# Group sums in parts, two tiles written in parts, and a new written-out order in a two-layer spectral-filter and GLU kernel

## The chip, the cores and the metric

The kernel runs on one core of one Trainium2 chip. The metric is the device time of one execution in microseconds (us), and a kernel's time is the median of several runs. Before the change the median of three runs is 1050.22 us (1048.97 to 1051.25).

The engines are named as the profile names them: PE is TensorE, DVE is VectorE, ACT is ScalarE, POOL is GpSimd, SP is SyncE, which only issues transfers here.

## The reference

Two kinds of layer alternate, twice each, on `x` of 2048 x 512 numbers in float32:

```
x = x + A(layernorm(x))    A: X = rfft2(x) over both axes; X = X * (w_r + 1j * w_i); irfft2(X)
x = x + B(layernorm(x))    B: ((x W_gate) * (x W_up)) W_down,  512 -> 1792 -> 512
x = x + A(layernorm(x))
x = x + B(layernorm(x))
```

The same weights serve both times. The change is in A; B fills most of the time.

## The kernel before

`x` is kept on chip in `xs`, as 16 tiles of 128 x 512. "Layer 0" and "layer 1" below are the first and the second pair of A and B.

A transforms in stages. **Tiles.** For each of the 16 tiles, VectorE or ScalarE computes the layernorm's mean and spread, ScalarE scales the tile's transform matrix by it (`tws` in layer 0, `tw` in layer 1), and TensorE makes the tile's product `tp` (`fwd_rest`, L469). The result goes into a big array E of 128 x 4 x 16 x 16 x 8: blocks, tiles, groups, columns of a group. Tiles marked "P" in `FOLD` are halved ahead by GpSimd (`fo`), and ScalarE copies their product to E in one 128x512 copy. Tiles marked "Q" (2, 5, 8, 11 and 14 of layer 0) are halved after the product: ScalarE copies one half to `tb`, and VectorE writes the sum and the difference with `tb` to E, 128x256 each. Tile 15 is copied in two parts, the columns of groups 0 and 1 (64) first or last and those of groups 2 to 15 (448), which `cuts` in `fwd_rest` says.

**Groups.** E is then read across the tiles. For each of the 16 groups, `middles` (L529) makes two sums `fs`: halves of E added and subtracted, 128x256 each, read for all 16 tiles. So the first sum of a group needs all 16 tiles in E. Groups 0 and 1 (`FAST`) are summed by VectorE, the others by GpSimd. TensorE multiplies them (`dp`, eight 64x128 products for each group, two records each in the profile), ScalarE copies the result (`zs`), TensorE transforms again (`zp`), VectorE and GpSimd multiply with the filter (`wq`, loaded by SyncE; GpSimd adds a 128x8 correction to each piece), TensorE transforms back (`vq`), and ScalarE copies it into E over the group. Groups go to TensorE in the sets of `TWOS`: 0 alone, then pairs. **Inverse tiles.** Then each tile is transformed back (`yi`, `yo`), added to `xs`, normalised (`xn`) and transposed (`tq`) for B, whose products `gx` to `gz`, `ex` to `ez` and `db` fill TensorE for hundreds of microseconds. Layer 1's tile products run largely woven into layer 0's B.

What sets the order: every operation is first recorded in a list with what it reads and writes, and `Plan.order` (L268) then replays that list in the order of a table, `ORDER`, which a program has worked out ahead and which is stored compressed; `PLACES` gives each temporary its buffer. The instructions of one engine run in that order, and an instruction waits until the engines that it depends on have got far enough. So a wait at the head of an engine's queue also holds what stands behind it. Buffers are rings: 18 temporaries of 128 x 512, eight banks for the results of products. Every instruction is issued through one helper class, `Queue`, whose line, L314, is therefore the line of nearly every row of the profile; rows are told apart by the tiles that they name.

At the start TensorE runs `WARM` (6) idle products of 128x512 and one of 128x256 on zeros (`wp<-warm`), before the first tile is ready. Between tiles and groups it runs one more idle product (`idle`, L524, `wp<-midt`).

Of the kernel before, what the change touches and what calls it, by code (L numbers as in the profile page):

```python
# [103 lines left out]
FAST = (0, 1)  # L104
TWOS = [(0,)] + [(g, g + 1) for g in range(1, 15, 2)] + [(15,)]
# [14 lines left out]
    'mA)yv(X1R#89tT6z8G{oKwKY`m8|JQq}s|Jy^QYX^$ziAf}Eu~S|;mQaq-#7^JV3A?IBBamF&>lL^xKe$!ebI!tUF&BmOKZ(d<!@`>oL?PA2O6*q5*2_$V9Sox<;KuUJXsbAnXonO-uE'  # L120
    '7|hiX@~WN*-<f+&`%6QaLR{nVew4(6u%hy`t_E52Z3k0@?;~}tRAi^W_&ZYP5H0uZE)q}bE4n~Rf$Cha6e}+BcXfo0XHA?$fUvQ6>nmL^ZS_}auFK>XeOiu#gl2qpnGquy`jYODJniN!'
    '@Qd)iTOI-V&zWrdI~dL)I?js;nrL=wDZMOJiFpYvYNBPGz9n0bP)BBKNj)m<q^>NpSJ0{pIQ|?&wUc_}%_e(Hx|^SEJGo$+g{1p?^ny3pPvc1=Ps$f)_!)WD7lf_TDq6(cw5`p2ogs5{'
    'g;oH4ZKXdr>?yBkKVq4o=WKanvExattmTczlMA#Pk=mwT%0fNPZe64dE9Ynn*~-6CGD<hda6To;e~8Z`(nE&u-hw)CRp#4z(v&QHR?d6(@_Vt1uc7*o36%r3mT8BCwHhXcw754^U)81('
    '#+7;IE89(mT4UNsbJ;F&`n^6Ztz|4Za$RDH%#Ru>7D?gKU3!6z2~?NGVDJMpy>InK{Sj1bCF>W7hXr+AKFCz<jE6hubZM-!C5`V#L2+eJc|bQwD}4&7i$G{aDMH4$JBPI~Pv(+=A##M*'
    'AISJwGE{%ngLqA~J6d_fC=<l&(HHRFU1WvhgJ|ORv>ql#xAZH#QW34%;)!9%OC%#U>ML?kBjf>Dtk20OSh!P%@ccI2E^ksP7DyzL?_pVnyst0GcSw1Ty7CY8?hP=Lt5?yrF<JMXHs|$0'
    'RwPh$rh@(t@k2#y*$$>kn7g3AusPsYFs=p{lL5r3C4TnM@isVeahz|q+D*FEPB2@@*@L#Ec~(|n?=eaD8<|`QQ7cPBM&+H9)3yp8J*r8@w}m8EA~Z|GOg^8lkt5~gjFi`fwxJhE-tW*n'
    '`P<f&({j(om}D~co)pkO@$3V}uy&6vYS#JfyaTqO$)|pO4qC#&%VrHVp5{w^WOguXeZ{}k$=Rto9Di=r>MCZg|E{?pLXWA4{Nj3pI$&6nq6a|YaT{gwY?3K0SM;<^Hs>_gRyAkU+NNd~'
    'NchfHGV~W4XCm?W4f}{mCmW7xaV<>+z9c#J7P1;3bGbeWR`aQt*QqV>`1vCB<OV&*Ros<20klSG1UsFuC%D#KmXUL1Kwku}M$V9lE2%?2bLV#(Z?=*Pk>q3-d04)&E#-4+tI(<Hm^_`w'
    'y7Tr0JHl&4hs~!tAJd`!Chre+iUsFC+a4xSrrOud8`?kznf=5tLyuV_Pf!7jq?#u3G4I3h-WufAmf3i?HI=m{$SWuL_BlJtt10D(<`ytuWIa{*wk`oL>-8BrO9cKtL!2tmy(UW^`?z@;'
    'l#T%xe-gLFc8FQ4Ep;Uo>`Sc$#+KN>wY^!QFVj!9YgwYuMJC%(cv}3UUPrE7VTV;j?{BJ58mR3@CrJdW4}p%pGSH4OY5F*t46tL(Hgr%>U61FUk!S2eb3(_nq9YyuPd!IGE@&I_cR2|B'  # L130
    'UYk)1%gbBXJJ2{=dfO-&V^-657TO#zw#}^9_w6|Doxqb;Pm+Hz=<={s*0r*cI$cC+5TBED;j>6@DQmcv4Enm#VV3G;JJg)UYs>M@DRo@rq<&!MnLgCPM%1ULOm#ZJCOUfx{9`5^us>IS'
# [1055 lines left out]
```

## Time and profile before

| | us |
|---|---|
| median of 3 runs (lowest, highest) | 1050.22 (1048.97, 1051.25) |
| profiled execution: its own time | 1049.96 |
| profiled execution: span of the records | 1048.2 |
| busy in the span: PE matmul | 1032.4 |
| PE weight load | 900.8 |
| DVE | 803.6 |
| POOL | 747.0 |
| ACT | 421.0 |

The span runs from the first to the last record; the execution's own time has 1.76 us more around it. Busy time is summed over the records of an engine; weight loads run beside products, so PE's two shares overlap. In the timelines a row is a run of like instructions: start, time from the first start to the last end, engine, what is written `<-` what is read, the shape, how many (`x4`), and in brackets how long the engine stood idle before it and what released it. The tables of stretches also give PEclk, the granted clock of TensorE as a share of full speed; it is 1.00 in every stretch shown.

### The profile page before, as it was taken

Reading aid. Unit: us, or ns where it says so; the run is one execution under the profiler, and the core shown is the slowest. Engines: PE = TensorE matmul, PEld = TensorE weight load, DVE = VectorE, ACT = ScalarE, POOL = GpSimd, SP = SyncE. Lnnn points to the kernel's source line nnn. Section 1 sums busy time; section 2 is a strip of 40 time slices with the busy share of each in tenths; the row PEclk is TensorE's granted clock in tenths of the full one; section 3 lists DMA queues with packets and bytes.
Section 4 is the critical chain, followed back from the end, with each engine's and each line's share of the span. In section 5 each row is a group of like instructions: output and inputs, shape, how many; then the busy total and the mean of one; then the engine's idle time right before and its main releaser. Section 6 shows DMA issues by size and latency. Waiting matters only on the chain.

```text
span 1048.2 us, 18805 instructions
## 1 busy us (share of the span) xinstructions
PE 1032.4 (98%) x6560; PEld 900.8 (86%) x6560; DVE 803.6 (77%) x1581; ACT 421.0 (40%) x1011; POOL 747.0 (71%) x960
## 2 busy tenths in 40 slices
...
GB/s 360 224 83 191 64 218 229 234 214 277 253 213 140 278 215 158 201 164 230 120 319 78 6 12 201 153 176 176 190 275 219 91 222 220 162 211 179 213 141 81
DMA packets 129469, 193.66 MB, mean 185 GB/s; under 512 B 39264, under 2 KB 50784, under 8 KB 127328
## 3 DMA queue, kind: packets, MB, share of 16 engines
...
q14 instruction: 41, 0.34, 0.1%
...
## 4 chain that ended last, share of the span: by engine, by line
PE 90%; DVE 6%; POOL 1%; ACT 1%; DMA 1%; issue 1%; SPq 0%; DVEq 0%; POOLq 0%; ACTq 0%
PE gz L314 15%; PE gx L314 15%; PE db L314 8%; PE gy L314 7%; PE gw L314 7%; PE gv L314 7%; PE ex L314 5%; PE ez L314 5%; PE ey L314 3%; PE dp L314 3%; PE ev L314 3%; PE vq L314 3%; PE ew L314 3%; PE zp L314 2%; DVE xs L314 2%; PE yi L314 2%
## 5 line engine op out<-in xcount | busy, mean ns | idle before, releaser
L314 PE MATMUL gx<-xA,wt 128*128 128x512 f32 (+1 forms) x852 | 179.3, 346 | 0.0
L314 PEld LDWEIGHTS gx<-xA,wt 128*128 128x128 f32 x852 | 137.9, 190 | 17.9
L314 POOL TENSOR_TENSOR sf<-q,sf 128x256 fp32r<-128x256 f32 x99 | 73.0, 742 | 106.4 <-ACT sf L314 97.3
L314 POOL TENSOR_TENSOR sf<-cc,sf 128x256 fp32r<-128x256 f32 x97 | 71.7, 742 | 55.8 <-ACT sf L314 48.9
L314 DVE TENSOR_TENSOR xs<-xs,db 128x512 f32<-128x512 f32 x128 | 85.5, 681 | 23.1 <-PE db L314 22.6
L314 PE MATMUL db<-wd,h 128*128 128x512 f32 x336 | 91.1, 392 | 0.1
L314 PE MATMUL gy<-xS,wt 128*128 128x512 f32 (+1 forms) x426 | 89.9, 346 | 0.0
L314 PE MATMUL gz<-xS,wt 128*128 128x512 f32 (+1 forms) x426 | 89.9, 346 | 0.0
L314 PE MATMUL gz<-xA,wt 128*128 128x512 f32 (+1 forms) x426 | 89.6, 346 | 0.0
L314 PE MATMUL gw<-xS,wt 128*128 128x512 f32 (+1 forms) x426 | 89.5, 346 | 0.0
L314 PE MATMUL gv<-xS,wt 128*128 128x512 f32 (+1 forms) x426 | 89.4, 345 | 0.0
L314 ACT COPY s<-gx 128x512 f32<-128x512 f32 (+1 forms) x71 | 35.2, 496 | 132.0 <-PE gx L314 131.7
L314 PEld LDWEIGHTS gz<-xS,wt 128*128 128x128 f32 x426 | 69.0, 189 | 9.5 <-DVE q L314 0.4
L314 PEld LDWEIGHTS gw<-xS,wt 128*128 128x128 f32 x426 | 69.1, 189 | 9.1
L314 PEld LDWEIGHTS gz<-xA,wt 128*128 128x128 f32 x426 | 69.0, 189 | 9.0
L314 PEld LDWEIGHTS gv<-xS,wt 128*128 128x128 f32 x426 | 69.0, 190 | 9.0
L314 PEld LDWEIGHTS gy<-xS,wt 128*128 128x128 f32 x426 | 68.6, 190 | 8.6
L314 DVE TENSOR_TENSOR q<-gy,s 128x512 f32<-128x512 f32 (+1 forms) x71 | 41.0, 577 | 45.2 <-PE gy L314 33.0
L314 ACT CAST sf<-q 128x256 fp32r<-128x256 f32 x99 | 40.0, 407 | 82.0 <-DVE q L314 41.5
L314 PEld LDWEIGHTS db<-wd,h 128*128 128x128 f32 x336 | 61.1, 188 | 11.6 <-POOL h L314 0.2
L314 POOL TENSOR_TENSOR wt<-rg,wt 128x512 fp32r<-128x512 f32 (+1 forms) x56 | 64.2, 1158 | 5.2 <-ACT wt L314 5.1
L314 PE MATMUL ex<-bf,sf 128*128 128x256 f32 x396 | 58.1, 283 | 0.0
...
## 6 DMA issues: line engine op xcount, KB each, us to landing
...
```

The source lines that it names most:

```text
L314: ins = f(*args, **kw)
```

## The change

- `PARTED` and `LATE` are new: the sums of groups 0, 1 and 2 are made in two operations each, one over tiles 0 to 13 (128x2x112 in the order, 224 columns), one over tiles 14 and 15 (128x2x16, 32 columns). Each part waits only for the tiles that it reads. So these three groups have twelve operations in place of six in each layer.
- Tile 14, as tile 15 already, goes to E in two parts, groups 0 and 1 apart from the rest. In layer 0 it is a "Q" tile, so VectorE writes it in four operations instead of two. In layer 1 its two copies are made by VectorE, not ScalarE.
- `WARM` goes from 6 to 5: one 128x512 idle product fewer at the start.
- `ORDER` and `PLACES` are replaced as a whole; all instructions may stand elsewhere in their queue.

```diff
--- before.py
+++ after.py
@@ -102,6 +102,7 @@
 FOLD = "PPQPPQPPQPPQPPQP", "PPPPPPPPPPPPPPPP"
 SWAPS = "12" * 8, "12" * 8
 FAST = (0, 1)
+PARTED, LATE = (0, 1, 2), 14
 TWOS = [(0,)] + [(g, g + 1) for g in range(1, 15, 2)] + [(15,)]
 SPLIT = True, True
 POOLED = ((1, 0), (2, 0), (3, 0)), ((0, 1), (1, 0), (1, 1), (2, 0), (2, 1), (3, 0))
@@ -113,94 +114,95 @@
 I2A, I2B, XOFF, XSTEP = 3.0, 4.0, 2.0, 5.0
 ASTEP, BSTEP, ASLIP = 1.5, 2.8, 6.0
 ORDER = (
-    'c-lRh37n7B_s7qDW-&92F=mLdj2Zhr)<MaVeNBpFDYRNDm8C>zv4m2Qq<&Gf$d-MVtT7D3*mpk)5zP!^=DFwpzK{MtUcSro+~?f0e9k$abH79iit;B)ZfQ};(R*4zjAUssxvM$aPzuNa'
...
+    'c-lRh2Y6P+5{75bpAbk$fDjO*h29~QP(^wX1f+KrMNqISh>DGRDT;C}h!+qLq$30Y!Ap}8N+5*Zs{tg^A%x`Y+;@+9A0Ga4&Ys=bZ@!uNX8(xf7Q?^Xa!2#aeZ8+y5-Gku<WpgZkn8$D'
...
 PLACES = (
-    '00000000000001000001020000031211300214304145000065715000616000817a090071100b11000c0110de0f1g20e0h010023201560437102b9f0ad01000c8g02h1201400f'
...
+    '000000000000011200000100112323043010000414050065000517001600610782170013900a300c110001e10bd1fg020hb4100506022510470gc019d708a0e0210f8h192040'
...
 
 BLOCKS = 160
 STAGE = "POOL"
-WARM = 6
+WARM = 5
 EARLY = 0
 CLEAR = 1.5
 SLOTS = 5
@@ -486,11 +488,12 @@
                 TE.matmul(tp()[:, 128 * b:128 * b + 128], rows()[:, b], tw(), start=True, stop=True, skip_group_check=True)
 
         pe(0.9, spread, [*src, tw], [tp, *(["idle"] if t == 15 else [])])
-        cuts = ((0, 2), (2, 16)) if t == 15 else ((0, 16),)
+        cuts = ((0, 2), (2, 16)) if t >= LATE else ((0, 16),)
         key = lambda n, *k: (E, t, "fast", *k) if n < len(cuts) - 1 else (E, t, *k)
         if early:
             for n, (a, b) in enumerate(cuts):
-                act(32 * (b - a), lambda a=a, b=b: A.copy(E()[:, :, t, a:b], tp().rearrange("p (b g e) -> p b g e", b=4, e=8)[:, :, a:b]),
+                by, copy = (dve, V.tensor_copy) if not tws and t == 14 else (act, A.copy)
+                by(32 * (b - a), lambda a=a, b=b, copy=copy: copy(E()[:, :, t, a:b], tp().rearrange("p (b g e) -> p b g e", b=4, e=8)[:, :, a:b]),
                     [tp], [key(n)], due=due)
             return
         t4 = lambda b, lo, hi: tp()[:, 128 * b:128 * b + 256].rearrange("p (b g e) -> p b g e", b=2, e=8)[:, :, lo:hi]
@@ -527,17 +530,21 @@
             pe(cols / 595, lambda bk=bk: TE.matmul(bk()[:, 0:cols], midt[:, 0:128], midt[:, 0:cols], start=True, stop=True), ["midt"], [bk, key])
 
     def middles(gs, E, df, W, due, swaps):
-        fss, dps = [], []
+        fss, dps, parts = [], [], []
         for g in gs:
-            src = lambda j, g=g: E()[:, :, :, g].rearrange("p (a j) t e -> p a j t e", j=2)[:, :, j]
-            es = [k for t in range(16) for k in (((E, t, "fast"), (E, t, "fast", 0)) if t == 15 and g in FAST else ((E, t), (E, t, 0)))]
+            cuts = ((0, LATE), (LATE, 16)) if g in PARTED else ((0, 16),)
+            src = lambda j, lo, hi, g=g: E()[:, :, lo:hi, g].rearrange("p (a j) t e -> p a j t e", j=2)[:, :, j]
             fs = temp("fs", "f", (128, 4, 16, 8))
-            for i, op in ((0, ALU.add), (1, ALU.subtract)):
-                args = [*es], [(fs, i), (E, "g", g, i)]
-                if g in FAST:
-                    dve(256, lambda i=i, op=op, fs=fs, src=src: tt(fs()[:, 2 * i:2 * i + 2], src(0), src(1), op), *args, two=True)
-                else:
-                    pool(256, lambda i=i, op=op, fs=fs, src=src: gtt(fs()[:, 2 * i:2 * i + 2], src(0), src(1), op), *args)
+            for n, (lo, hi) in enumerate(cuts):
+                es = [k for t in range(lo, hi) for k in (((E, t, "fast"), (E, t, "fast", 0)) if t >= LATE and g in FAST else ((E, t), (E, t, 0)))]
+                for i, op in ((0, ALU.add), (1, ALU.subtract)):
+                    args = es, [(fs, i, n), (E, "g", g, i)]
+                    sums = lambda f, i=i, op=op, fs=fs, src=src, lo=lo, hi=hi: f(fs()[:, 2 * i:2 * i + 2, lo:hi], src(0, lo, hi), src(1, lo, hi), op)
+                    if g in FAST:
+                        dve(16 * (hi - lo), lambda sums=sums: sums(tt), *args, two=True)
+                    else:
+                        pool(16 * (hi - lo), lambda sums=sums: sums(gtt), *args)
+            parts.append([(fs, i, n) for i in range(2) for n in range(len(cuts))])
             fss.append(fs)
             dps.append(bank("dp", "x" if g and g == gs[0] else "a"))
 
@@ -550,7 +557,7 @@
                         TE.matmul(dp()[64 * c:64 * c + 64, o:o + 128], f4[:, j, :, q], df()[:, j], start=True, stop=True,
                                   skip_group_check=True)
 
-        pe(0.83 * len(gs), features, [*((fs, i) for fs in fss for i in range(2)), df, *(["idle"] if gs[0] == 0 else [])], dps)
+        pe(0.83 * len(gs), features, [*(k for ks in parts for k in ks), df, *(["idle"] if gs[0] == 0 else [])], dps)
         for g, dp in zip(gs, dps):
             middle(g, dp, E, W, due(g), swaps[g])
```

What this makes of the queues is shown at three places. In the names, a number after an underscore tells buffers apart, and is another one in each version. The first is VectorE's queue in layer 0, from the last tile writes to the last sum; before, `fs_464` is group 0 and `fs_467` group 1, and `tp_394` is tile 14:

```order
L314 TENSOR_TENSOR E_132<-tp_394,tb_430 128x2x128
L314 TENSOR_TENSOR E_132<-tp_277,tb_418 128x2x128 x2
L314 TENSOR_TENSOR E_132<-tp_360,tb_407 128x2x128
L314 TENSOR_TENSOR E_132<-tp_394,tb_430 128x2x128
L314 TENSOR_TENSOR fs_464<-E_132 128x256 x2
L314 TENSOR_TENSOR fs_467<-E_132 128x256 x2
```

and with the change, where `fs_471` is group 0, `fs_456` group 1, and `tp_397` tile 14:

```order
L316 TENSOR_TENSOR E_132<-tp_379,tb_411 128x2x128 x2
L316 TENSOR_TENSOR E_132<-tp_364,tb_402 128x2x128 x2
L316 TENSOR_TENSOR fs_456<-E_132 128x2x112 x2
L316 TENSOR_TENSOR E_132<-tp_397,tb_425 128x2x16
L316 TENSOR_TENSOR E_132<-tp_397,tb_425 128x2x112
L316 TENSOR_TENSOR E_132<-tp_397,tb_425 128x2x16
L316 TENSOR_TENSOR fs_471<-E_132 128x2x112 x2
L316 TENSOR_TENSOR fs_456<-E_132 128x2x16 x2
L316 TENSOR_TENSOR fs_471<-E_132 128x2x16 x2
```

Group 1's large parts now stand ahead of the last three writes of tile 14, and group 0's sums and the four short parts behind them; before, all four sums stood behind all writes, group 0 first.

The second is GpSimd's queue at the same place; before, with group 2 as `fs_462`:

```order
L314 TENSOR_TENSOR fs_462<-E_132 128x256 x2
L314 TENSOR_TENSOR fs_483<-E_132 128x256
L314 TENSOR_TENSOR fs_505<-E_132 128x256
L314 TENSOR_TENSOR fs_507<-E_132 128x256 x2
L314 TENSOR_TENSOR fs_483<-E_132 128x256
L314 TENSOR_TENSOR fs_505<-E_132 128x256
L314 TENSOR_TENSOR fs_541<-E_132 128x256
```

and with the change, with group 2 as `fs_464`:

```order
L316 TENSOR_TENSOR fs_464<-E_132 128x2x112 x2
L316 TENSOR_TENSOR fs_464<-E_132 128x2x16 x2
L316 TENSOR_TENSOR fs_495<-E_132 128x256
L316 TENSOR_TENSOR fs_518<-E_132 128x256 x2
L316 TENSOR_TENSOR wq_124<-wq_124,hp_71 128x8
L316 TENSOR_TENSOR fs_495<-E_132 128x256
L316 TENSOR_TENSOR fs_534<-E_132 128x256
L316 TENSOR_TENSOR fs_536<-E_132 128x256
```

Group 2's two sums have become four, whole sums of later groups follow, and a 128x8 addition to a filter piece now stands among them.

The third is VectorE's queue in layer 1; before, where `fs_6411` is group 0, `fs_6413` group 1:

```order
L314 TENSOR_SCALAR rs_6364<-rs_6364 128x1
L314 TENSOR_SCALAR rs_6364<-mv_6357,rs_6364 128x1
L314 TENSOR_SCALAR rs_6364<-rs_6364 128x1
L314 TENSOR_TENSOR fs_6411<-E_4950 128x256
L314 TENSOR_TENSOR fs_6413<-E_4950 128x256
L314 TENSOR_TENSOR fs_6411<-E_4950 128x256
L314 TENSOR_TENSOR fs_6413<-E_4950 128x256
L314 TENSOR_TENSOR zp_6457<-zp_6457,wq_6112 128x512
```

and with the change, where `fs_6413` is group 0, `fs_6399` group 1, and `tp_6393` tile 14:

```order
L316 TENSOR_TENSOR fs_6399<-E_5259 128x2x112
L316 COPY E_5259<-tp_6393 128x4x16
L316 COPY E_5259<-tp_6393 128x4x112
L316 TENSOR_TENSOR fs_6413<-E_5259 128x2x112 x2
L316 TENSOR_TENSOR fs_6413<-E_5259 128x2x16 x2
L316 TENSOR_TENSOR fs_6399<-E_5259 128x2x112
L316 TENSOR_TENSOR fs_6399<-E_5259 128x2x16 x2
L316 TENSOR_TENSOR zp_6467<-zp_6467,wq_6120 128x512
```

One large part of group 1 stands first, VectorE's two copies of tile 14 follow, then all of group 0, and the rest of group 1 last.

## Rows read from the trace of the kernel before

**Rows 1.** The page, part 1: busy us, share of the span, instructions.

```profile
PE 1032.4 (98%) x6560; PEld 900.8 (86%) x6560; DVE 803.6 (77%) x1581; ACT 421.0 (40%) x1011; POOL 747.0 (71%) x960
```

**Rows 2.** The table of stretches, TensorE: columns in its first line.

```profile
core 0: us, PE busy (x), PEclk, DMA share, GB/s
...
25.60:32.10 6.50, 4.03 (x52) 1.00 1.01 418
...
84.00:98.00 14.00, 11.51 (x67) 1.00 0.47 151
...
125.00:525.00 400.00, 400.00 (x2273) 1.00 0.62 207
...
544.20:548.20 4.00, 3.17 (x20) 1.00 1.02 412
...
598.00:625.00 27.00, 24.82 (x160) 1.00 0.05 15
...
```

**Rows 3.** The waits, TensorE: us in total, times, longest us.

```profile
PE dp L314 <- DVE fs L314: 3.1, 3, 1.7
```

**Rows 4.** The timeline, TensorE, 25 to 33 us: start, us, work, [idle before].

```profile
25.47 1.02 PE L314 MATMUL wp<-midt 128*128 128x512 f32 x2
28.24 1.10 PE L314 MATMUL dp<-df,fs 128*64 128x128 f32 x16 [1.75 <-DVE fs L314]
30.07 1.97 PE L314 MATMUL dp<-df,fs 128*64 128x128 f32 x32 [0.72 <-DVE fs L314]
```

**Rows 5.** The timeline, VectorE, layer 0.

```profile
24.90 0.42 DVE L314 TENSOR_TENSOR E<-tp,tb 128x256 f32<-128x256 f32 x1
26.35 3.58 DVE L314 TENSOR_TENSOR fs<-E 128x256 f32<-128x256 f32 x4 [1.03 <-ACT E L314]
```

**Rows 6.** The timeline, GpSimd, layer 0.

```profile
26.33 8.26 POOL L314 TENSOR_TENSOR fs<-E 128x256 f32<-128x256 f32 x11 [3.02 <-ACT E L314]
```

**Rows 7.** The timeline, ScalarE, layer 0.

```profile
24.26 1.10 ACT L314 COPY E<-tp 128x512 f32<-128x512 f32 x2
25.67 0.58 ACT L314 COPY E<-tp 128x512 f32<-128x512 f32 x1 [0.31 <-PE tp L314]
```

**Rows 8.** The timeline, VectorE and GpSimd, layer 1.

```profile
546.47 0.42 DVE L314 TENSOR_TENSOR fs<-E 128x256 f32<-128x256 f32 x1 [2.51 <-ACT E L314]
546.47 0.76 DVE L314 TENSOR_TENSOR fs<-E 128x256 f32<-128x256 f32 x2 [2.51 <-ACT E L314]
547.14 1.81 DVE L314 TENSOR_TENSOR fs<-E 128x256 f32<-128x256 f32 x2
546.95 5.33 POOL L314 TENSOR_TENSOR fs<-E 128x256 f32<-128x256 f32 x7 [1.88 <-ACT E L314]
```

**Rows 9.** The tile fs, by engine: duration ns min/median/max, first and last start.

```profile
L314 POOL TENSOR_TENSOR fs<-E x56: 716/733/906, 26.3 to 574.4; 128x256 f32<-128x256 f32 x56
L314 DVE TENSOR_TENSOR fs<-E x8: 418/942/984, 26.3 to 548.0; 128x256 f32<-128x256 f32 x8
```

**Rows 10.** Groups by form, GpSimd, 24 to 50 us: busy us, mean ns.

```profile
L314 POOL TENSOR_TENSOR wq<-wq,hp 128x8 f32<-128x8 f32 x5 | 1.0, 236 | 0.0
```

**Rows 11.** The timeline, ScalarE and TensorE, layer 1.

```profile
544.30 2.58 ACT L314 COPY E<-tp 128x512 f32<-128x512 f32 x6
546.37 1.12 PE L314 MATMUL wp<-midt 128*128 128x512 f32 x2 [0.19 <-ACT E L314]
548.14 2.93 PE L314 MATMUL dp<-df,fs 128*64 128x128 f32 x48 [0.64 <-DVE fs L314]
```

**Rows 12.** The chain of waits, the start: start us, us, what.

```profile
2.12 7.63 DMA xs<-in_x_dram
13.14 0.41 ACT tws L314
13.64 12.01 PE tp L314 x104
```

**Rows 13.** The timeline, TensorE, end of the inverse tiles of layer 1.

```profile
616.15 1.13 PE L314 MATMUL yi<-di,E 128*128 128x128 f32 x8 [0.80 <-DVE mv L314]
```

More of the change, by code (lines that the diff above doesn't have):

```diff
@@ L120 @@
[L120 to L131, printed above, removed]
@@ L140 @@
-    '{akJMni}Bi`#KYy4R?q6^K4j10b)0w-P854{AwYqq_chu;+o|b4yl9W9r<NL7SVT&ESKc`Xg-hPYDRwPkXz{Wjtpeyv2c)SQae8)<aZfH#aDGK`YNnAL*IkZB+6Wwz$6e32YQbxT1n<f'
-    'f4u4u7u8GfmQYZxOdvhw1E#mpvWV6BWQ^;l3OgML+co?>2721TxHD`Ga|K2^PBUz6qs%Bf=nIMT$XYT-UV<roK`q%wuRZEl@ea{@ZrJ)}q4d!Q;aBPK!9$t?mg|y9m4dxPWvYzC_u<^B'
-    'D%0f+%|O;Prm@M=1QxbSQbFt#DMA#*?jW|;$k|G^jk!uc&DNeF4au+(bp6+ux2(3%ZSs`-gas|=bsu2iNd1s~YVj={_W6Z=&b~G9RUw%Dc4n|W@)39%OuY7BX{zo+ihEbBVipqntM&kM'
-    '=PPu<&!jVZeg+RcC&}=yf-($#T#d^42~%B1b#uiz>V>P)omufI>(}TY-e2a4L$HCB+E2d)MaAiWp2X<iWaQWMqL=g{H6~vt!f)xTbT2ob+(cqovO7xJb8iI*dK>0lmsxO<?v;TOO{IvI'
@@ new lines @@
+    'zSA~RkzJhBIB|G%mvvf;U5w4uHLF<g^bL^snbkj*)gYT+wrM#jiVtEyD^B+6L48(E>lfNny2viQ36fRh2cD_Sp7Tq(p3)xpumS%INPBkqgKm-E^bX_V@c&J{tQ}>aZq&{o5-aOXH+w_R'
+    '=p4`}2yPLQp*cDRERKQX1?;GgwKuea^wv)qaWU9kDfm?keCx7@^X%kzaEg;II-mP3S-GUN)8+U)jc=*iU)M1<3Qrc4d-$xsZiIyw^hI4N#iW+*ke0fZJF&cPlo2{jZm45YZg%}4YkUjt'
+    '$skjb`$ObuuEz3hvOOjn@a=U*hQY#o_}cLODcOz9cfm__m&R#%ldOd_1ALBYtQIlRQXB7VV*EM~DyXNW9ak3HKS8GxV{Yhs;8R}K+S82dX6{;dw{h6KoOal?#GB|Rg+}N6sJApxzSOch'
+    '!EDjf;Ccj%Gw|A8Y#eRR$s$S7Z?q~L`A*)o<xF|lcEVOMTZx`9=_*TLp08{4Dd{Y)!>eJSxJe5#-w<sgmGJ6tVqlZjF$Ziut!awljj#1}*@}Or%St>r0PnVt4zfnK>0X|%ATw=C(_LQH'
@@ new lines @@
+    '`sT1--&oxa{y*C(W`q8!&GA}YDHophu!Naw|Es>XH|uRvP<jf!ZPY$8Ps^Hk{SCXUK0yQ;St74U4PDEMeWV}pUr9FW8{F-!UFAoeEbr?w@z`-4>CTnf*gT)8PQ$a`N^e;Nf7i(yx(pPm'
+    '@zhaftSoQJEZxJWO89UeBXYxqY9NshHdmG?O_h*LlbWpaIZ--Io3cVJIYNBx0@;JS?<c4AB)?2&-FarbjU*mll{YmU&kvIQ#N;zUrU;X&@&)r8BEFS~36os%K$`1T?akd382_|X;VC17'
+    '@oYZEDfgO_x1PZEKCo>GHl5eswV`~bU5LUIJmWFf6dh;EV*N=iDlORmN!!=BwP&%fUb0xb6Bk>9e3wsJ%6MDZ<T0165`%^uc}{QJT3(3UGs%2pciKK?vp#CJ`Nd2bv)vzPh&p-CEFsS-'
+    'yt)eS>%z+il7}3dMYKJT92?CmH3QB?nB2^no0W^oIk{y^$V2X2wXra+h;D{!MqYx0b;0;sTf;QdUF;#-rsz;J!GFRlCcoR_<|1*nlU%)+_$zKMX>m2?G^{<N%IgJdOi3_{Cx(3+Z_aC$'
```

139 lines of the change are left out of this document (74 added, 65 removed).

## The prediction

> **What bounds the kernel now.** Read the busy shares first: TensorE is busy for 98% of the span, every other engine for 77% or less [rows 1]. Then ask in which stretches TensorE is not full [rows 2]. From 125 to 525 us it is busy for all of 400.00 us, so no reordering there can gain anything, only lose. It is not full in 25.60 to 32.10 (4.03 of 6.50 us), in 84 to 98 (11.51 of 14.00), in 544.20 to 548.20 (3.17 of 4.00) and in 598 to 625 (24.82 of 27.00). The first and the third are where layer 0 and layer 1 go from the tile products `tp` to the group products `dp`, and this is where the change works. The waits of TensorE by releaser give the name: `dp` waits for sums `fs` of VectorE three times, 3.1 us together [rows 3].
>
> Layer 0, row by row [rows 4]: an idle product ends at 26.49, `dp` of group 0 starts 28.24 (1.75 late), the next two groups start 30.07 (0.72 late) and end 32.04. VectorE starts its four sums at 26.35 and needs 3.58 us [rows 5], GpSimd starts at the same moment and runs eleven in 8.26 us [rows 6]. Both start when ScalarE has copied the last tile to E, 25.67 to 26.25 [rows 7].
>
> The price of a sum is the point of the case. In layer 1 VectorE starts first: its first two sums come 0.34 apart, and the first takes 0.42; the two that run beside GpSimd's take 1.81 together [rows 8]. Over the whole run VectorE's eight lie between 418 and 984 ns, GpSimd's fifty-six between 716 and 906 [rows 9]. So beside each other one sum of each passes in about 0.9 (four in 3.58), neither engine gets two in a row, and a sum of VectorE costs more than twice what it costs alone. The Trainium skill, page "SBUF — State Buffer", section "SBUF: two separate sides", calls this an exclusive lock: whichever of a VectorE operation with two SBUF inputs and a GpSimd operation starts first has the shared ports "for the whole instruction". By that alone a pair would take 0.34 + 0.67 = 1.01 (0.67 for GpSimd's alone, worked out below); the trace has 0.9, so the turns agree and the price is a little less.
>
> **The change, part by part.** All sums are made against the profiled execution, 1049.96 us, which is 0.26 under the median of the three runs, 1050.22.
>
> *Layer 0, sums in parts.* The twelve small and large operations replace six; which is late now?
> (1) Start. The early parts need tiles 0 to 13. ScalarE's queue ends in one whole copy more than before (the copy of an early tile is put off), then the copy of tile 13, then tile 15. Two copies end at 25.36, 0.55 each [rows 7], so tile 13 is in E between 25.36 and 25.91. I take 25.7, against 26.3 before.
> (2) The two early sums of group 1 on VectorE and the two of group 2 on GpSimd take turns: two pairs at 0.9 x 7/8 = 0.79, to 27.3.
> (3) VectorE now writes the remaining three parts of tile 14, of which two are tiny: one full write takes 0.42 [rows 5], so 0.4 to 0.6, to 27.8. Queued behind them are group 0's sums, and GpSimd's late parts wait for the same writes.
> (4) Group 0's early sums: 0.34 each alone, 0.79 each in turns: 0.7 to 1.6. GpSimd has only its two short late parts at that moment, so 0.9, to 28.7.
> (5) The four late sums of VectorE, 1/8 of a sum in size. No row shows one. Below, they cost 0.1 each, next to GpSimd's 128x8 operation of 0.24 [rows 10]; above, each waits for one whole GpSimd sum, 0.67 (7 of the 11 in [rows 6] ran without VectorE beside them: (8.26 - 4 x 0.9) / 7). That is 0.4 to 2.7. GpSimd's next instructions are three whole sums, one 128x8 addition and a fourth sum, so not all four can meet a whole one. I take 1.3, near the middle: 30.0.
> Then the three groups' `dp` run without a gap in 2.93 [rows 11] to 32.9, against 32.04: **0.9 lost**. The ends: earliest start with all cheap, 25.4 + 1.6 + 0.4 + 0.7 + 0.4 = 28.5, three groups done at 31.4, 0.6 gained; latest, 25.9 + 1.6 + 0.6 + 1.6 + 2.7 = 32.4, done at 35.3, 3.3 lost. The reason that so little comes of it: group 0, which TensorE asks for first, stands behind group 1 and tile 14 on VectorE, and TensorE gets all three at once where it had the first at 28.24.
>
> *Layer 1, sums in parts and tile 14 by VectorE.* ScalarE makes six copies from 544.30 to 546.88 there [rows 11], VectorE has nothing to do from 543.95 to 546.47 (2.51 idle [rows 8]). Now the early sums of group 2 and one of group 1 run in that hole, VectorE takes over both copies of tile 14 (some 0.6) in the hole too, and ScalarE is free of one. Group 0's early sums end at about 546.5, its two late ones need the small copy of tile 15, which follows that tile's product, at about 546.3 (the idle product behind it starts at 546.37 now), and GpSimd has nothing to run then: ready at 546.7. The idle product, which waits for VectorE's copy and the last tile, ends at about 547.1 (1.02 as in [rows 4]). So `dp` starts at 547.1, not 548.14 [rows 11]: **1.0 gained**. Ends: 1.1, when nothing follows late, or 0, when VectorE's early sum is held up by GpSimd and pushes tile 14 and all behind it by 0.9. The rest of group 1 (one large, two small sums) falls beside GpSimd's whole sums, which can cost up to 0.6 of it by what it makes the second and third group wait.
>
> *One idle product fewer at the start.* These products are not on the chain of what ended last. It goes from the DMA of x (2.12 to 9.75) to a scaling by ScalarE, and `tp` waits for that until 13.64 [rows 12]. Cover: that DMA. If the scalings came earlier the product would have cost up to 1 us; they don't. 0, ends -0.3 to +0.3. The granted clock stays 1.00 in all stretches of [rows 2]; at the start TensorE has work in either version.
>
> *Both parts of tiles 14 and 15.* VectorE has two operations more in layer 0, which are in (3), and ScalarE one copy fewer in layer 1, as above; nothing else. SyncE's queue: `wq` and `tw` loads stand in another order, with nothing waiting on them at 26 to 48. 0.
>
> *The order elsewhere.* In 598 to 625 TensorE waits 0.80 for VectorE before the third `yi` [rows 13]; the new order puts that product ahead of `gx`, with nothing between it and what it waits for, and lets the next ones follow: 0.4 gained, ends -0.5 to +0.8. The stretch 84 to 98 hangs on GpSimd's queue, whose instructions are the same ones: 0, ends -0.5 to +0.5. In the full stretches only a new wait can come: 0.2 lost, ends 0 to 1.0.
>
> **Sum:** -0.9 + 1.0 + 0.4 - 0.2 = 0.3 gained, **1049.7 us**. Called no change: a measurement of this kernel can tell about 0.2%, here 2.1 us, so 1048.1 to 1052.3 reads as the same.
>
> **The rivals.**
> A. *Short sums slip in.* The late parts cost 0.1 each and take no turn; group 0 is ready at 28.5 to 28.9. Layer 0 gains 0.2 to 0.6, layer 1 1.1, the other stretches 0.8: 2.3, so 1047.7. For it: an eighth of a sum holds the ports for little, and GpSimd is itself waiting for tile 14 just before. Against: turns were strict for all six sums of VectorE that met GpSimd [rows 5, 8].
> B. *Every sum waits its turn* (slower). GpSimd's short late parts finish before VectorE is done with tile 14, so that each of group 0's six sums, large or small, meets a whole sum of GpSimd. Place: 27.8 to 33; price 6 x 0.9 = 5.4 in place of my 2.2. `dp` starts at 33.2, three groups done 36.1: 4.1 lost. With layer 1's gain cut to 0.6 by the same turns and 0.2 from the rest: 1053.3. It makes the run slower than 0.2% from about `dp` at 32.4 on in layer 0 (32.4 + 2.93 - 32.04 = 3.3, less 1.0). The page named above gives this case by its lock, for a small operation as for a large one. For it: the rows of turns; against: one of GpSimd's next five instructions is 128x8, and its short parts wait for tile 14 as well.
> C. *The order elsewhere decides.* Of TensorE's 15.8 us without work (1048.2 - 1032.4) the two places hold 3.1; 84 to 98 alone holds 2.49, 598 to 625 2.18 [rows 2]. A new order can give back 2 to 3 of these 4.7 or add as much: about 1047.2 or 1052.2. For it: every instruction may have moved; against: the sets of instructions there are the same and the chain is GpSimd's and VectorE's own work.
>
> **How the numbers follow.** My forecast (layer 0 a loss of 0 to 2, layer 1 a gain) 0.50; A 0.18; B 0.14; C 0.18, half each way, and only half of each half over the threshold. Faster by over 0.2%: A 0.18 + C 0.05, and 0.03 of the forecast's tail: 0.26. Slower: B 0.13 + C 0.05: 0.18. Within: 0.56. The range runs from A and C's good side, a little under 1047.7, to between C and B: 1047.0 to 1052.4.
>
> **What would show it.** In layer 0: early sums of both engines from 25.4 to 25.9 on, VectorE's in about 0.8 each; its four short sums the last before `dp`, each 0.1 to 0.7 long; the three `dp` without a gap, starting at 30.0 (28.5 to 32.4). In layer 1: GpSimd's first sum near 544.6, `dp` at 547.1. TensorE's other waits as before. The forecast is wrong if `dp` of layer 0 starts before 28.5 or after 32.4, if `dp` of layer 1 doesn't start by 548.1 on the old time scale, or if a wait over 1 us stands in a stretch that was full.

## The result and the profile after

| | before | after |
|---|---|---|
| median of 20 runs each (lowest, highest), us | 1049.53 (1048.76, 1052.99) | 1052.16 (1050.98, 1054.02) |
| ratio to before, 95% interval | | 1.0023 (1.0017 to 1.0029) |
| profiled execution: own time / span, us | 1049.96 / 1048.2 | 1051.58 / 1049.5 |

The change costs 2.4 us by the ratio, where the prediction gave 1049.7 and "no change". The two profiled executions differ by 1.6. TensorE's busy time hardly moved (part 1 of the page after, [rows 1]):

```profile
PE 1031.3 (98%) x6558; PEld 900.8 (86%) x6558; DVE 806.3 (77%) x1593; ACT 423.2 (40%) x1010; POOL 748.5 (71%) x964
```

What grew is its time without work, from 15.8 to 18.2 us. The longest waits that differ, TensorE after (total us, times, longest):

```profile
PE tp L316 <- ACT tws L316: 3.3, 2, 1.8
PE wp L316 <- DVE E L316: 1.3, 1, 1.3
PE tp L316 <- POOL fo L316: 1.1, 1, 1.1
PE dp L316 <- DVE fs L316: 0.4, 1, 0.4
```

The wait that the change was to shorten, `dp` for sums [rows 3], fell from 3.1 to 0.4. But `tp` now waits 3.3 for scaled transform matrices: 1.79 before the first tile's products, which start at 9.50 (10.03 before, behind idle products), and 1.50 before the last set. The timeline of TensorE after, layer 0 (12.55 is the second set of tile products, 24.41 the last):

```profile
12.55 3.22 PE L316 MATMUL tp<-tws,fo 128*128 128x128 f32 x24 [1.06 <-POOL fo L316]
...
24.41 4.20 PE L316 MATMUL tp<-tws,fo 128*128 128x128 f32 x32 [1.50 <-ACT tws L316]
29.87 1.12 PE L316 MATMUL wp<-midt 128*128 128x512 f32 x2 [1.26 <-DVE E L316]
31.42 2.94 PE L316 MATMUL dp<-df,fs 128*64 128x128 f32 x48 [0.42 <-DVE fs L316]
```

Before, in the same view, the last tile products:

```profile
21.88 3.76 PE L314 MATMUL tp<-tws,fo 128*128 128x128 f32 x32
```

They ended at 25.64; now they end at 28.61, 2.97 later. The three `dp` [rows 4] end at 34.36 instead of 32.04, 2.32 later. So the loss lies ahead of the sums, and the sums give 0.65 back. What holds the last products? The timeline of ScalarE and VectorE after:

```profile
23.87 0.40 ACT L316 ACTIVATE tws<-tws,rs 128x128 f32<-128x128 f32 x1 [2.03 <-DVE rs L316]
20.64 2.26 DVE L316 TENSOR_SCALAR hp<-hp 128x32 f32<-128x32 f32 x1
22.81 0.32 DVE L316 TENSOR_SCALAR rs<-mv,rs 128x1 f32<-128x1 f32 x2
25.69 2.38 DVE L316 TENSOR_TENSOR E<-tp,tb 128x256 f32<-128x256 f32 x7 [1.03 <-ACT tb L316]
28.17 1.15 DVE L316 TENSOR_TENSOR fs<-E 128x224 f32<-128x224 f32 x2
29.25 0.57 DVE L316 TENSOR_TENSOR E<-tp,tb 128x32 f32<-128x32 f32 x3
29.74 1.72 DVE L316 TENSOR_TENSOR fs<-E 128x224 f32<-128x224 f32 x6
```

`tws` waits for `rs` of VectorE, and `rs` stands behind a scaling of `hp` (half of the filter's correction, multiplied by -1 in place) that takes 2.26 us. Before it took 0.17 (timeline of VectorE before):

```profile
21.96 0.17 DVE L314 TENSOR_SCALAR hp<-hp 128x32 f32<-128x32 f32 x1
```

And GpSimd, after and then before:

```profile
6.41 0.74 POOL L316 TENSOR_TENSOR fo<-xs 128x256 f32<-128x256 f32 x1 [0.47 <-DMA xs<-in_x_dram]
9.71 13.14 POOL L316 TENSOR_TENSOR fo<-xs 128x256 f32<-128x256 f32 x19 [2.56 <-DMA xs<-in_x_dram]
```

```profile
5.15 4.14 POOL L314 TENSOR_TENSOR fo<-xs 128x256 f32<-128x256 f32 x6 [3.90 <-DMA xs<-in_x_dram]
9.81 2.10 POOL L314 TENSOR_TENSOR fo<-xs 128x256 f32<-128x256 f32 x3 [0.52 <-DMA xs<-in_x_dram]
...
18.07 3.52 POOL L314 TENSOR_TENSOR fo<-xs 128x256 f32<-128x256 f32 x5 [0.17 <-DMA xs<-in_x_dram]
```

Two moves of the new order stand here. The scaling of `hp` stood behind the end of GpSimd's halvings (21.59); now it is ready at 20.64, 2.21 before they end (22.85), and it ends with them. And GpSimd idles 2.56 up to 9.71: its queue has the second halving of tile 4, which needs a transfer, ahead of halvings of tiles 1 and 3 that are ready.

Layer 1 went as meant (TensorE, then VectorE, after):

```profile
546.85 2.02 PE L316 MATMUL tp<-tw,fo 128*128 128x128 f32 x16 [0.59 <-ACT tw L316]
548.97 1.10 PE L316 MATMUL wp<-midt 128*128 128x512 f32 x2
550.00 2.84 PE L316 MATMUL dp<-df,fs 128*64 128x128 f32 x48
```

```profile
547.28 0.88 DVE L316 TENSOR_TENSOR fs<-E 128x224 f32<-128x224 f32 x1 [0.64 <-ACT E L316]
548.08 0.74 DVE L316 COPY E<-tp 128x64 f32<-128x64 f32 x2
548.75 1.39 DVE L316 TENSOR_TENSOR fs<-E 128x224 f32<-128x224 f32 x7
```

From the last products' start to `dp` it takes 3.15, before 3.98 (544.16 to 548.14 [rows 11]): 0.83 gained. The inverse tiles of layer 1 (598 to 625 in [rows 2]) stand some 1.7 us later now, so they are compared from their first `yi` to their last: 594.07 to 627.66 before, 595.83 to 629.27 after, 0.15 gained. The wait of 0.80 [rows 13] is gone, but two others stand near it:

```profile
611.71 1.10 PE L316 MATMUL yo<-vs,tw 128*128 128x512 f32 x2 [0.79 <-DVE rs L316]
...
614.53 3.21 PE L316 MATMUL yi<-di,E 128*128 128x128 f32 x24 [0.69 <-DVE xs L316]
```

### The profile page after: what moved, and what is told of

Its sections match the earlier page's. It is cut to its first block, busy times and chain, and to the rows that moved or that the text cites. A ratio compares the mean times of both kernels' runs of the same rounds, so it can differ in the third digit from the quotient of the medians.

```text
span 1049.5 us, 18807 instructions
## 1 busy us (share of the span) xinstructions
PE 1031.3 (98%) x6558; PEld 900.8 (86%) x6558; DVE 806.3 (77%) x1593; ACT 423.2 (40%) x1010; POOL 748.5 (71%) x964
## 4 chain that ended last, share of the span: by engine, by line
PE 89%; DVE 8%; ACT 1%; issue 1%; DMA 1%; POOL 1%; SPq 0%; DVEq 0%; ACTq 0%; POOLq 0%
PE gz L316 14%; PE gx L316 14%; PE db L316 8%; PE gy L316 7%; PE gv L316 7%; PE gw L316 7%; PE ex L316 5%; PE ez L316 5%; DVE xs L316 3%; PE ey L316 3%; PE ev L316 3%; PE vq L316 3%; PE ew L316 3%; PE dp L316 2%; PE zp L316 2%; PE yi L316 2%
## 5 line engine op out<-in xcount | busy, mean ns | idle before, releaser
L316 POOL TENSOR_TENSOR sf<-q,sf 128x256 fp32r<-128x256 f32 x91 | 67.2, 742 | 71.0 <-ACT sf L316 71.0
L316 ACT CAST sf<-q 128x256 fp32r<-128x256 f32 x91 | 36.6, 407 | 71.4 <-PE ez L316 21.6
L316 ACT CAST sf<-cc 128x256 fp32r<-128x256 f32 x98 | 39.6, 406 | 56.9 <-PE ew L316 14.5
```

Source lines behind the costliest of these rows:

```text
L316: ins = f(*args, **kw)
```

## The experiments

Theory: two instructions that the new order moved, VectorE's scaling of `hp` and GpSimd's halving of tile 4, cost what was lost, and the sums in parts gain. Rival: the sums in parts, or the order as a whole, lose. All moves use one addition to `Plan.order`; `put(i, j)` sets operation i behind operation j.

```diff
+        turn = [int(i) for i in turn]
+        def put(i, after):
+            turn.remove(i)
+            turn.insert(turn.index(after) + 1, i)
...
```

**Undo one move, or both.** In the changed kernel 20 is the scaling, 158 the last scaling of an `rs`, 81 the halving of tile 4, 65 one of tile 3.

```diff
 e1_scale_later
+        put(20, 158)
 e2_tile4_later
+        put(81, 65)
 e3_both, e16_both_again
+        put(20, 158)
+        put(81, 65)
```

> The changed kernel, with one VectorE instruction moved: the scaling of hp (128x32, SBUF to SBUF), which took 2.26 us at 20.64 there and 0.17 in the kernel before, goes behind the last statistics of the tiles, where GpSimd's tile sums are over. Theory 1 (this instruction is held until GpSimd's row of sums is empty, and ScalarE's scalings and TensorE stand behind it): it takes about 0.2 us, TensorE's wait of 1.50 before the last tile products goes, the three first group products end about 1.5 us earlier than 34.36; 1.5 us faster than the changed kernel, about 1050.7. Rival 2 (the loss is the group sums in parts, which take turns with GpSimd's): the end of the group products stays near 34.4 or moves by under 0.5; about 1052. Rival 3 (the instruction waits for something else, its data or a queue slot): it takes as long at its new place.

> The changed kernel, with one GpSimd instruction moved: the second half of tile 4's first sum, which waits for a transfer of x until 9.71 there with four ready sums of tiles 1 and 3 behind it, goes behind these four. The scaling of hp stays where it is. Theory 1: GpSimd's idle 2.56 us shrink to about nothing, its tile sums end about 2 us earlier than 22.85, TensorE's wait of 1.06 before 12.55 goes, and since GpSimd's row is empty earlier, the scaling of hp is held for little too: both losses go, some 2.5 us faster than the changed kernel, about 1049.7. If the scaling is held whatever GpSimd does: 1.0 faster, about 1051.2. Rival 2 (turns of the parted sums): under 0.5 faster.

> The changed kernel with both moves. Theory 1: as with tile 4's sum moved alone, or up to 0.3 us better; about 1049.5, level with the kernel before or a little under, since layer 1's group products and the inverse tiles gained 1.1 together. Rival 2: under 0.5 faster than the changed kernel, about 1051.9.

> The changed kernel with both moves again, to say with more runs whether it beats the kernel before: from its first median a ratio of 0.9996, from the trace 0.2 us gained in layer 0 and 0.6 in layer 1, so 0.9992 to 0.9998; rival: no difference, 0.9998 to 1.0005.

Against the kernel before on the same chip: the scaling last 1.0002 (0.9993 to 1.0011); tile 4 later 1.0000 (0.9992 to 1.0009); both 0.9996 (0.9987 to 1.0004), and again 1.0008 (0.9999 to 1.0017). So either move undone takes the loss away, and that both together do better than one cannot be measured. (`e3` and `e16` are one kernel; 3 of 11 executions of the first and 6 of 11 of the second have a mean clock of 0.998 or less.) With the scaling last (its tile's rows, then TensorE):

```profile
L327 DVE TENSOR_SCALAR hp<-hp x1: 172/172/172, 22.6 to 22.6; 128x32 f32<-128x32 f32 x1
```

```profile
22.51 4.11 PE L327 MATMUL tp<-tws,fo 128*128 128x128 f32 x32
27.87 1.12 PE L327 MATMUL wp<-midt 128*128 128x512 f32 x2 [1.25 <-DVE E L327]
29.41 2.94 PE L327 MATMUL dp<-df,fs 128*64 128x128 f32 x48 [0.42 <-DVE fs L327]
```

`dp` comes 2.01 sooner than in the changed kernel (31.42). With tile 4 later alone the scaling stays where it was, ready at 20.43 in the middle of a GpSimd instruction, and takes only 0.565: it was released at that instruction's end, though GpSimd worked on until 23.05. So there the hold went away with the other move. GpSimd's row there:

```profile
16.77 6.28 POOL L327 TENSOR_TENSOR fo<-xs 128x256 f32<-128x256 f32 x9 [1.48 <-DMA xs<-in_x_dram]
```

**The halving of tile 4 alone, in the kernel before.**

```diff
 e11_tile4_earlier (kernel before)
+        put(82, 67)
```

> The kernel before, with GpSimd's second operation of tile 4 ahead of the ready ones of tiles 0 and 1. Theory (it waits for its DMA until 9.7 us and holds those up): GpSimd idle about 2.5 us up to 9.7, the first tile products later, twelve tiles' products done 0.5 to 1.0 later, ratio 1.0003 to 1.001. Rival (the start hangs on the DMA of x anyway): no move of the later products, ratio 0.9995 to 1.0003.

1.0028 (1.0019 to 1.0037): more than expected. GpSimd and TensorE there, and two rows of the table of stretches:

```profile
9.62 13.78 POOL L325 TENSOR_TENSOR fo<-xs 128x256 f32<-128x256 f32 x20 [2.94 <-DMA xs<-in_x_dram]
```

```profile
13.12 3.31 PE L325 MATMUL tp<-tws,fo 128*128 128x128 f32 x24 [3.13 <-POOL fo L325]
...
29.76 1.10 PE L325 MATMUL dp<-df,fs 128*64 128x128 f32 x16 [1.75 <-DVE fs L325]
31.59 3.60 PE L325 MATMUL dp<-df,fs 128*64 128x128 f32 x32 [0.72 <-DVE fs L325]
```

```profile
25.00:30.00 5.00, 3.25 (x26) 2.43 (x26) 3.76 (x8) 2.33 (x6) 2.15 (x3) 1.00 1.03 419
30.00:35.00 5.00, 4.28 (x48) 3.85 (x44) 1.44 (x2) 0.59 (x1) 5.00 (x8) 0.67 1.02 428
```

Tile 4 ahead of ready work costs 1.52 there (`dp` at 29.76 against 28.24 [rows 4]), with the scaling at 0.17. The clock can account for the rest of the 2.9 us: it is 0.67 of full speed from 30 to 35, so that 32 records of `dp` take 3.60 instead of 1.97 in the profiled execution. All nine executions have a mean clock of 0.998 or less; of the 28 of the kernel before beside them, five.

**Sums in parts against whole sums,** in the changed kernel with both moves:

```diff
 e7_whole_sums
+        put(20, 158)
+        put(81, 65)
+        put(257, 243)
+        put(256, 257)
...
-                    sums = lambda f, i=i, op=op, fs=fs, src=src, lo=lo, hi=hi: ...
+                    at, to = (lo, hi) if len(cuts) == 1 else (0, 16 * n)
+                    sums = lambda f, i=i, op=op, fs=fs, src=src, lo=at, hi=to: ... if hi else None
```

The last two moves put group 0's sums ahead of group 1's in layer 0; each whole sum stands where the late part stood.

> The changed kernel with both moves (1049.4), and the sums of groups 0, 1 and 2 made whole again, behind all writes, group 0 first, in both layers; the writes of tiles 14 and 15 stay in parts. Theory 1 (the parts gain): layer 0's three group products end 0.6 later against the last tile product, layer 1's start 0.8 later; 1.4 us slower than with parts, about 1050.8. Rival 2 (in layer 0 the parts lose 0.9 by taking turns, in layer 1 they gain 1.0): level, about 1049.4.

1.0017 (1.0008 to 1.0027), against 0.9996 and 1.0008 with parts: parts are worth some 1.6 us (1.0017 less the mean of the two, 1.0002), give or take about 1 us by the intervals. TensorE with whole sums, and with parts (`e3_both`):

```profile
21.84 4.20 PE L330 MATMUL tp<-tws,fo 128*128 128x128 f32 x32 [0.17 <-ACT tws L330]
...
30.49 1.97 PE L330 MATMUL dp<-df,fs 128*64 128x128 f32 x32 [0.73 <-DVE fs L330]
...
546.17 2.02 PE L330 MATMUL tp<-tw,fo 128*128 128x128 f32 x16 [0.51 <-ACT tw L330]
551.08 1.97 PE L330 MATMUL dp<-df,fs 128*64 128x128 f32 x30 [0.37 <-DVE fs L330]
```

```profile
21.91 4.20 PE L328 MATMUL tp<-tws,fo 128*128 128x128 f32 x32 [0.17 <-ACT tws L328]
28.91 2.94 PE L328 MATMUL dp<-df,fs 128*64 128x128 f32 x48 [0.42 <-DVE fs L328]
...
544.72 2.02 PE L328 MATMUL tp<-tw,fo 128*128 128x128 f32 x16 [0.59 <-ACT tw L328]
547.87 2.85 PE L328 MATMUL dp<-df,fs 128*64 128x128 f32 x48
```

From the last tile products to the end of three `dp`: layer 0 10.62 whole, 9.94 in parts (0.68 gained); layer 1 6.88 and 6.00 (0.88). Together 1.56, in keeping with the times.

**The sixth idle product.**

```diff
 e12_six_idle (with put(20, 158) and put(81, 65))
+        put(5039, 4)
...
+    pe(0.86, lambda: TE.matmul(wp(), warm()[:, 0:128], warm(), start=True, stop=True), [warm], [(wp, 7)])
```

> The changed kernel with both moves (scaling of hp last, tile 4's second operation later) and the sixth idle product put back, behind the other five. The prediction held it at 0 (-0.3 to +0.3): the wait of tp near 9.7 us shorter by its 0.9 to 1.0, everything behind it unmoved, ratio within 0.0003 of the same kernel with five (0.9996). Rival (it keeps the clock from falling later, or it delays): ratio off by over 0.0006 either way.

1.0003 (0.9995 to 1.0011), between the two results without it: no difference that can be measured. But the product did not get its old place: it ran behind the first tile's products, and the wait before them, which was expected to shrink, did not (2.93, against 2.66 in `e3_both`). TensorE there:

```profile
9.80 1.13 PE L330 MATMUL tp<-tws,fo 128*128 128x128 f32 x8 [2.93 <-ACT tws L330]
10.77 3.33 PE L330 MATMUL wp<-warm 128*128 128x512 f32 x4
```

In this execution the granted clock was 0.66 from 10 to 15 us, behind that wait. So the run says that one idle product more costs or gains nothing there; what it was worth in its old place is not shown.

**How long is a scaling held, and by what?** First elsewhere: the scaling in two other places of the kernel before (21 is the scaling there, 20 its load), and fifteen operations of its size spread over GpSimd's halvings in the changed kernel with the scaling last, as scalings in place and as sums of two operands.

```diff
 e4_scale_earlier (kernel before)
+        put(20, 17)
+        put(21, 172)
 e8_scale_mid (kernel before)
+        put(20, 22)
+        put(21, 112)
 e5_probe_scalings (with put(20, 158))
+        put(5039, 69)
... (fourteen more, 5040 to 5053)
+    for n in range(15):
+        dve(32, lambda: V.tensor_scalar(probe[:, 1], probe[:, 1], -1.0, None, op0=ALU.mult), [], ["probe"])
 e6_probe_sums (with put(20, 158) and the same fifteen places)
+        dve(32, lambda: tt(probe[:, 1], probe[:, 0], probe[:, 1], ALU.add), [], ["probe"])
```

> The kernel before, with the scaling of hp put amid GpSimd's row of eight tile sums (12.37 to 17.91), its transfer issued early enough for that. Theory 1 (held until the row is empty): it takes 1.5 to 2.3 us and ends when GpSimd's eighth sum does, near 18; TensorE gets a wait of 0.5 to 1.5 before tile products that had none; 0.5 to 1.5 us slower than the kernel before. Rival 4 (it waits for one GpSimd instruction, as the group sums do): it takes at most 0.9 us, and the time moves by under 0.3.

> The kernel before, with the scaling of hp and its transfer early enough that it stands at about 14.6 us, with four or five of GpSimd's tile sums still to come in one row (to 17.8). Theory 1a (it can lose at several instruction changes): 0.6, 1.3, 2.0, 2.7 or 3.2 us long; at 2 us or more TensorE waits 1 us or more for ScalarE's scalings, and the kernel is 1 us slower than before. Theory 1b (one instruction is waited for): at most 0.9 us long and within 0.3 us of the kernel before.

> The changed kernel with the scaling of hp out of the way, and fifteen extra scalings of the same kind (128x32, in place, by a constant) put among VectorE's tile statistics, where GpSimd's tile sums follow each other without a gap. Alone one takes 0.17 us. Theory 1a (VectorE loses at some of GpSimd's instruction changes): durations scatter from 0.2 to over 2 us, in steps of GpSimd's 0.69. Theory 1b (one GpSimd instruction is waited for, never two): none over about 0.9 us, and the 2.26 us of the changed kernel had another cause. Its time says nothing: VectorE has more to do.

> The same fifteen places, with small sums of two SBUF operands (128x32) in place of the scalings. If all instructions that need the shared ports take turns as the group sums did: each waits for the rest of one GpSimd instruction, 0.2 to 0.9 us, none longer. If sums and scalings are alike and scatter: some over 1 us.

In the kernel before the scaling took 0.31 at 17.44 and 0.53 at 14.54, at ratios of 0.9996 (0.9987 to 1.0005) and 1.0008 (0.9999 to 1.0017). The first came in the last instruction of a row of GpSimd, which ended at 17.72, so it could not have been held for longer; only the second tells. The fifteen (duration min/median/max):

```profile
L343 DVE TENSOR_SCALAR probe<-probe x15: 161/247/733, 10.1 to 23.5; 128x32 f32<-128x32 f32 x15
```

```profile
L343 DVE TENSOR_TENSOR probe<-probe x15: 167/218/812, 10.1 to 23.8; 128x32 f32<-128x32 f32 x15
```

GpSimd's instructions follow each other every 0.69 (13.09 for 19 in either run). Fourteen of the fifteen scalings meet that row; they end where one of its instructions ends and wait for one at most; one of the sums passed the end of one and waited for the next. Then the changed kernel again, and its place varied: 177, 175 and 135 are operations on `rs` beside it.

```diff
 e9_change_again (the changed kernel itself)
 e10_scale_one_place
+        put(20, 177)
 e13_scale_03_earlier
+        put(20, 175)
 e14_scale_01_later
+        put(20, 135)
 e15_probe_in_place (5039 is one scaling of another tile, as in e5; in e17 and e18 too)
+        put(5039, 20)
+        put(20, 158)
 e17_one_probe
+        put(20, 158)
+        put(5039, 90)
 e18_probe_ahead
+        put(5039, 90)
```

> The changed kernel itself, for a second profile of it. If the long scaling of hp (2.26 us in the first profile) comes from where it stands beside GpSimd's work, it is there again: 1.5 to 2.9 us, ending with GpSimd's 128x256 row, and the time is 1.0020 to 1.0026 of before. If it was a chance of one execution, it takes at most 0.75 and the ratio falls to about 1.0005.

> The changed kernel with the scaling of hp one place later on VectorE (behind one operation on 128x1). Theory of the exact moment (the ordinary hold is one GpSimd instruction, here it met several by the moment at which it was ready): 0.2 to 0.75 us, and the ratio to before as with the scaling put last, about 1.000. Rival, the stretch (beside an unbroken row of GpSimd's operations a scaling is held to the row's end): 2.1 us again, ratio 1.002.

> The changed kernel with the scaling of hp three places earlier on VectorE, ready some 0.4 us sooner: in the middle of a GpSimd instruction (0.5 before it ends), where in the changed kernel it is ready 0.03 to 0.12 before one ends. Theory of the moment (a scaling that comes right before a boundary loses it and the next ones, one that comes in the middle passes at the first): 0.5 to 0.75 us, ratio near 1.0005. Rival, the stretch (what GpSimd does there holds any scaling to the end of its row): 2.6 us, ratio 1.002 or more.

> The changed kernel with the scaling of hp two places later, ready some 0.1 us after a GpSimd instruction has begun. Theory of the moment: it passes at the next boundary, 0.55 to 0.75 us, ratio near 1.0005. Rival, the stretch: held to the end of the row, 2.0 us, ratio 1.002.

> The changed kernel with the scaling of hp last (as in the run where it alone was moved) and, in its old place, a scaling of the same size of another tile that nothing reads. If the place and moment hold it: about 2.1 to 2.3 us, time as the changed kernel's (1.002). If it is something of hp itself (its DMA, its address, that GpSimd waits for it): at most 0.75 us, ratio near 1.000 to 1.0007.

> The changed kernel with the scaling of hp last and one scaling of another tile in the middle of GpSimd's unbroken row (near 14 us, row 9.5 to 22.6), the first operation of its kind since the row began. Theory of the unbroken row (GpSimd instructions that follow one another without a break pass the ports on among themselves, unless a scaling has broken in before): it is held to the row's end, some 8 us. Rival (something of the last three instructions of the row alone holds it): at most 0.75 us, as the fifteen in the run with fifteen.

> The changed kernel, the scaling of hp in its place, and one scaling of another tile ahead of it near 14 us. If an earlier scaling makes GpSimd give the ports up at each boundary from then on: the first takes what it takes, that of hp at most 0.75 us, ratio near 1.0005 or less. If the place alone counts: the first at most 0.75, that of hp 2.2 us again, ratio 1.002.

The tile's rows of `e9`, `e13`, `e14` and `e15`:

```profile
L326 DVE TENSOR_SCALAR hp<-hp x1: 2273/2273/2273, 20.4 to 20.4; 128x32 f32<-128x32 f32 x1
```

```profile
L327 DVE TENSOR_SCALAR hp<-hp x1: 2648/2648/2648, 20.0 to 20.0; 128x32 f32<-128x32 f32 x1
```

```profile
L327 DVE TENSOR_SCALAR hp<-hp x1: 2036/2036/2036, 20.6 to 20.6; 128x32 f32<-128x32 f32 x1
```

```profile
L329 DVE TENSOR_SCALAR probe<-probe x1: 2232/2232/2232, 20.7 to 20.7; 128x32 f32<-128x32 f32 x1
```

`e10` has 2.17 and `e18` 2.25. In all seven the scaling ends within 0.05 us of the end of GpSimd's row (for `e13`: row 9.47 to 22.60, scaling 19.99 to 22.64). So the hold is no chance of one execution, it does not hang on the moment within an instruction, and it is nothing of `hp`: a scaling of another tile at that place of this order waits until GpSimd pauses, too. The theory of the moment fell. The ratios agree: with a long hold 1.0025, 1.0020, 1.0026, 1.0022, 1.0032, 1.0023 and the changed kernel's 1.0023, mean 1.0024; changed orders without one (`e1`, `e2`, `e3`, `e12`, `e16`, `e17`) 1.0003 in the mean. The difference, 0.0021, is 2.2 us, the length of the hold.

The last two were to say why this place holds and the fifteen did not. The lone scaling of `e17` came at 12.77, 0.05 us before a GpSimd instruction began, and took 0.15; GpSimd's row went on for 9.6 us behind it. The one ahead in `e18` also took 0.15, and the scaling of `hp` behind it was held as ever. So an earlier scaling that passes freely, 7.4 us ahead, does not undo the hold. Why it lasts over three or four GpSimd instructions there stays open.

One thing does separate the cases on record, though no run varied it alone. Wherever a scaling was held to the row's end, GpSimd had worked for long without a pause and without a scaling of VectorE in between: 10.5 to 11.2 us in six profiles, 7.4 in `e18`. Where one passed at the first end of a GpSimd instruction while the row went on, it was 3.7 at most: up to 1.3 in `e5`, 2.3 in `e8`, 3.4 for the lone ones of `e17` and `e18`, 3.7 in `e2`. `e2` and `e13` are the closest pair: both ready within the same GpSimd instruction, 0.48 and 0.46 before the next one, 3.7 and 10.5 us into the row; one took 0.565, the other 2.65.

No version here beats the kernel before: the changed kernel with both moves stands at 0.9996 and 1.0008.

## Why the prediction was wrong, by its steps

The prediction said no change, 0.3 gained; measured were 2.4 lost. The time, 1052.16, still lies within the range given (1047.0 to 1052.4), but that is chance: the range's upper end was made of rivals B and C, and neither names the place of the loss.

**What failed: the start of layer 0 was costed at nothing.** The prediction says of the start that the idle product is covered by the DMA of x, and "If the scalings came earlier the product would have cost up to 1 us; they don't. 0, ends -0.3 to +0.3." It then prices the new order in 598 to 625, 84 to 98 and the full stretches, and has no term for 0 to 25.6 us, though VectorE, GpSimd and ScalarE all have queues there that were laid anew. It took the end of the last tile products from the old trace. That term was +2.97 in the profile: 0.88 up to the end of the first twelve tiles' products (22.91 for 22.03), the rest, 2.09, behind the held scaling. The experiments put 2.2 us of the result on the hold. Tile 4's halving counts too: with it later the hold was gone, and in the kernel before it cost 1.0028 by itself, part of that by the clock.

The means to see it were at hand: in VectorE's queue three operations on `rs` stand behind the scaling of `hp` before and eight now, in GpSimd's the halving of tile 4 has moved up, and [rows 9] show what a VectorE operation pays beside GpSimd. That a scaling with one operand pays as well was nowhere weighed.

**(1) Early sums at 25.7:** 28.17. Against the end of the last products it is 0.44 earlier (28.61), where the prediction had it 0.06 later (25.64): wrong through the start; relative to the products it came 0.5 sooner than predicted.

**(2) Two pairs in turns, 1.58 from 25.7 to 27.3:** 1.15 for VectorE's two. Mis-sized by 0.4: the first (0.39) began ahead of GpSimd's and did not wait, the second took 0.84.

**(3) Tile 14's parts, 0.4 to 0.6:** 0.57. Right.

**(4) and (5) Group 0's early sums 0.9 and the four late ones 1.3, 2.2 in all:** 1.72 for six. VectorE's eight sums in layer 0 by form:

```profile
L316 DVE TENSOR_TENSOR fs<-E x8: 177/384/843, 28.2 to 31.3; 128x224 f32<-128x224 f32 x4, 128x32 f32<-128x32 f32 x4
```

Group 0's two early sums (0.73 together) met only GpSimd's two short late parts, as the prediction has it. Of the four late ones three took 0.18 to 0.23; the third waited for a whole sum of GpSimd:

```profile
30.66 0.70 DVE L316 TENSOR_TENSOR fs<-E 128x32 f32<-128x32 f32 x1
```

So rival A's mechanism came for three of the four, and rival B, six turns of 0.9, did not come. The Trainium skill, page "SBUF — State Buffer", section "SBUF: two separate sides", would make the later of two wait for the whole of the other; the second early sum (0.84) and the late one of 0.70 agree, and for the others, which met short parts of GpSimd or the change from one instruction to the next, these rows do not decide.

From the last products' end to the end of three `dp`: 6.40 before, 5.75 now, 0.65 gained where the prediction had 0.9 lost. The sign of this step was wrong, and its size 1.5 off: 0.5 each from (1), (2) and from (4) with (5).

**Layer 1, 1.0 gained:** 0.83 in the profile, 0.88 by the whole sums. Right, a little smaller.

**One idle product fewer, 0:** no difference in `e12`, which has the product in another place, so this is not shown outright. The cover is not as predicted, with work for TensorE at the start in either version: TensorE now waits 1.79 us before the first tile's products.

**Order elsewhere:** 84 to 98 at 0: from the end of three `dp` to the first `gx` it takes 65.88 before and 66.02 after, 0.14 lost. Right. 598 to 625, 0.4 gained: 0.15. The wait that was priced went, as predicted, but others came near it, which the prediction gave no price. Full stretches, 0.2 lost: 0.23 from the first `gx` to the last products of layer 1, most of it a longer wait for `tw` there (0.59 against 0.38). Right.

The sum with the right terms: +2.97 (start) - 0.65 (sums of layer 0) + 0.14 (from `dp` to `gx`) + 0.23 (to the last products of layer 1) - 0.83 (sums of layer 1) - 0.56 (from there to the end) = +1.3, the difference of the spans. Of the 0.56, 0.15 are the inverse tiles and 0.3 one wait for `ev` near 1016 us (0.61 before, 0.31 after), which the prediction has no term for. By the ratio the loss is 2.4: the profiled execution before was 0.43 above its median, the one after 0.58 below, and these two traces do not show the difference. Of the rivals C came nearest, with its bad half (about 1052.2): the order decided, but in a stretch that C did not name.
